# Natural feature order for x and w1, and result products dealt to four strips

## The chip, the cores and the metric

The kernel runs on one core of a Trainium2 chip. The metric is the device time in microseconds (us). The engines named below are TensorE (PE; its weight loads appear as PEld), VectorE (DVE), ScalarE (ACT), GpSimd (POOL) and SyncE (SP), which here only issues DMA transfers. The profile is one profiled execution; its times count from the start of its span.

## The reference

Two blocks follow each other. The first is a gated linear recurrence over 768 steps for 4 batches and 8 heads of 48 features; the second is a mixture of four branches of two matrix products each, on 3072 rows of 384 features.

```python
# q, k, v, alpha: (B=4, H=8, S=768, D=48)
for t in range(S):
    state = alpha[:, :, t, :, None] * state + np.einsum('bhd,bhe->bhde', k[:, :, t], v[:, :, t])
    y[:, :, t] = np.einsum('bhd,bhde->bhe', q[:, :, t], state)
x = y.transpose(0, 2, 1, 3).reshape(B * S, H * D)        # (3072, 384)

# domain_probs: (3072, 4); w1: (4, 384, 1024); w2: (4, 1024, 384)
p = domain_probs / (domain_probs.sum(-1, keepdims=True) + 1e-09)
for e in range(4):
    h = np.maximum(x @ w1[e], 0.0)
    out += p[:, e:e + 1] * (h @ w2[e])
```

All inputs and outputs are 32-bit floats. A feature of x has the number 48 h + d, with head h and position d in the head.

## The kernel before

**Units.** The sequence is cut into 6 blocks of 128 steps. One block of one batch is a unit: 24 units, ordered by block and then by batch. For a unit, `attention` loads alpha, k, q and v (128 steps on the partitions, 8 heads beside each other), transposes the first three on TensorE in pairs of heads (L277), and builds in seven levels the matrix of decayed products of queries and keys for each head, `lat` (L348 to L428). VectorE's product of q and k, L298, serves its diagonal; L307 makes the scaled queries `QT`. `result` (L436 to L471) then forms the rows of x, transposed, in the PSUM tile `yps`: for each head, values times `lat`, and, after the first block, the carried state times `QT`. `yps` has 128 partitions and three pieces of 128 columns, so 384 features by 128 steps. ScalarE copies it into the operand of the first product (L467, L471). Then TensorE multiplies keys and values (L489), and VectorE updates the state `st` (L497 to L500). The last step asks for v of the unit after next (L502).

**Result products.** Each matmul of `result` has 32 columns of weights and fills a strip of 32 partitions of `yps`; four of them in a row fill the four strips. Before the change, the 384 features are permuted: pieces 0 and 1 of `yps` hold the first 32 positions of each of the eight heads, one head to a strip, and piece 2 holds the last 16 positions of all heads, a pair of heads to a strip. For this, v of the odd heads is stored with its last 16 positions first, in tiles of 64 elements a head (`values`, L128), the rest being zeros. A piece is finished before the next one begins, and within a piece all four strips first take the state with `QT`, then the values with `lat`.

**Branches.** The units form groups: the first of 2, then five of 4, the last of 2. For each group and each of the four branches e, `up` forms x times w1 in 8 chunks of 128 hidden features, ScalarE rectifies, and `down` multiplies by w2 (L663) and adds to the sums. The first group uses raw weights in 32-bit products (L562); later groups use weights split into parts (L570). ScalarE and VectorE make the parts in the background (`split_piece`, L233 to L239), GpSimd writes them to memory (`kept`, L240), and SP loads them again for the later groups (L203).

**Loads.** `load_piece` brings a quarter of w1 of one branch, 384 rows by 256 columns, into a tile of 128 partitions and three parts (L218 to L222). Since x is permuted, the rows of w1 are too: one transfer takes the first 32 rows of heads 0 to 3, one those of heads 4 to 7, and one the last 16 rows of all heads. Quarters of w2 come in one transfer each (L224). There are 16 quarters of w1; a branch's four are asked for during the branch before it, those of the first at the start, behind the loads of the first two units. `load` brings alpha, k and q in one transfer each (L174) and v in three (L179 to L181): even heads, last 16 positions of the odd heads, first 32 positions of the odd heads. All loads go through SP's queue, in the order in which the program asks for them. Each uses one of eight semaphores in turn, so SP holds a transfer back until the one eight places before it has landed; SP also waits until the buffer to be filled has been read.

**What sets the order.** The program is laid out by hand: each engine runs its instructions in the order in which they were recorded. `advance` and `deal` mix the steps of the units into the loops over the branches by planned times; these are constants in the code. At the start, `fill` puts in matmuls on zeros, and GpSimd clears tiles (L772 to L780).

Of the kernel before, what the change touches and what calls it, by code (L numbers as in the profile page):

```python
# [10 lines left out]
F32 = mybir.dt.float32  # L11
# [9 lines left out]
def kernel(  # L21
# [37 lines left out]
    nc = tc.nc  # L59

    B, H, S, D = q.shape
    E, DM, F = moe_w1.shape
    P = 128
    NCB = S // P
    NP = H // 2
    HD = 64
    QUAD = 32
    TAIL = D - QUAD
    KC = DM // P
    FCH = F // P  # L70
    NT = B * P
    NQ = 4
    QF = F // NQ
    FPQ = FCH // NQ
    LEVELS = [1 << i for i in range(7)]
    HALF = P // 2
    assert DM == H * D and S % P == 0 and D == QUAD + HD // 4 and H == 8 and DM == 3 * P and NT <= 512 and H % 2 == 0
    assert DM % P == 0 and F % (P * NQ) == 0 and DM <= 512 and KC * QF == FPQ * DM
    FINE = 1 + 1 / 4096
    TRIM = 1 - 1 / 8192  # L80
# [3 lines left out]
    j = np.arange(P)[:, None] % HALF  # L84
    n = np.arange(QUAD)[None, :]
# [4 lines left out]
    const = ctx.enter_context(tc.tile_pool(name="const", bufs=1))  # L90
# [15 lines left out]
    lat = const.tile([P, H, P], F32, name="lat")  # L106
# [18 lines left out]
    spare = hid.tile([P, 3, 2 * NT], F32R, name="hT", bufs=NQ)  # L125
    apart = {nm: spare[:, i, :H * HD].bitcast(F32).rearrange("p (h d) -> p h d", d=HD)
             for i, nm in enumerate("akq")}
    values = [const.tile([P, H, HD], F32, name=f"rv{i}") for i in range(2)]  # L128

    blocks = [const.tile([P, NP, 2, HALF], F32, name=f"qb{i}") for i in range(4)]  # L130
    free = deque(blocks)
# [1 line left out]
    def raw(u, nm):  # L133
        return values[u % 2] if nm == "v" else apart[nm] if u == 1 else early[nm]
# [32 lines left out]
    def load(u, names):  # L167
        if u >= len(units):
            return
        cb, b = units[u]  # L170
        for nm in names:
            src = srcs[nm][b, :, cb * P:(cb + 1) * P, :].rearrange("h s d -> s h d")
            if nm != "v":
                nc.sync.dma_start(out=raw(u, nm)[:, :, :D], in_=src)  # L174
                continue

            pairs = raw(u, nm).rearrange("p (a i) d -> p a i d", i=2)
            src = src.rearrange("p (a i) d -> p a i d", i=2)
            nc.sync.dma_start(out=pairs[:, :, 0, :D], in_=src[:, :, 0])  # L179
            nc.sync.dma_start(out=pairs[:, :, 1, :TAIL], in_=src[:, :, 1, QUAD:])  # L180
            nc.sync.dma_start(out=pairs[:, :, 1, TAIL:D], in_=src[:, :, 1, :QUAD])  # L181

    kept = [[dram.tile([P, 3, KC * QF], F32, name=f"kept{l}_{i}") for i in range(E * NQ)]
# [9 lines left out]
    def load_piece(l, i, beside=False):  # L195
        if i >= E * NQ * LAST:
            return
        gi, k = divmod(i, E * NQ)
        e, c = divmod(k, NQ)
        if gi > l:  # L200
            w = wt[l][i] = wts.tile([P, 3, KC * QF], F32R, name=f"w{l + 1}",
                                    bufs=AHEAD if l == 0 else NQ)
            nc.sync.dma_start(out=w.bitcast(F32), in_=kept[l][k])  # L203
            return
        if l == 1 and not beside:
            return
        if l == 0:

            if gi > 0 or e == 0:
                shared[c] = wts.tile([P, 3, KC * QF], F32R, name="w2", bufs=NQ)  # L210
            w = shared[c][:, 2 - e % 2 if gi == 0 else 2].bitcast(F32)
        else:

            place = (hidden[c][:, 0] if not split2(gi, e, c) else hidden[c + NQ // 2][:, 1])
            w = place.rearrange("p f n -> p (f n)")[:, :KC * QF].bitcast(F32)
        wt[l][i] = w
        if l == 0:
            heads = moe_w1[e].rearrange("(h d) f -> h d f", d=D)[:, :, c * QF:(c + 1) * QF]  # L218
            w = w.rearrange("p (c f) -> p c f", f=QF)
            for part in range(2):  # L220
                nc.sync.dma_start(out=w[:, part], in_=heads[part * H // 2:(part + 1) * H // 2, :QUAD])
            nc.sync.dma_start(out=w[:, 2], in_=heads[:, QUAD:])  # L222
        else:
            nc.sync.dma_start(  # L224
                out=w.rearrange("p (c d) -> p c d", d=DM),
                in_=moe_w2[e].rearrange("(c p) d -> p c d", p=P)[:, c * FPQ:(c + 1) * FPQ])
# [53 lines left out]
    def attention(u):  # L280
        cb, b = units[u]
        ra, rk, rq, rv = (raw(u, nm) for nm in ("a", "k", "q", "v"))
# [4 lines left out]
        QT = work.tile([P, NP, P], F32, name="QT")  # L287
        nc.scalar.copy(out=AT, in_=turned(pair(ra)))
        after = u + 2 if u == 0 else u + 1 if u > 1 else len(units)
        load(after, "a")  # L290
        yield
        KT = keys()
# [3 lines left out]
        def own_terms():  # L296
            own = work.tile([P, NT], F32, name="t")[:, :H * D].rearrange("p (h d) -> p h d", d=D)
            nc.vector.tensor_mul(own, rq[:, :, :D], rk[:, :, :D])  # L298
            nc.vector.reduce_sum(out=dot, in_=own, axis=AX.X)
            load(after, "k")  # L300
# [7 lines left out]
        if alone:  # L308
            own_terms()
        load(after, "q")  # L310
        yield

# [95 lines left out]
        for r in range(NP // 2):  # L408
            for s in range(2):
                nc.tensor.matmul(far[HALF * s:HALF * (s + 1), r],  # L410
                                 lhsT=KTs[6][:, 2 * r + s, :HALF], rhs=qbs[6][:, 2 * r + s],
                                 start=True, stop=True)
# [18 lines left out]

        st = sts[b]
        flat_st = st.rearrange("p a i d -> p a (i d)")
        flat_v = rv.rearrange("p (a i) d -> p a (i d)", i=2)

        def result():  # L436
            yps = ps.tile([P, KC, P], F32, name="yps", tag="w")
            for c in range(KC):


                if c < 2:
                    now = [[(2 * c + j // 2, j % 2, (0, HD + TAIL)[j % 2], 2 * QUAD * (j % 2))
                            for j in range(4)]]
                    turns = ([(True, now[0])] if cb > 0 else []) + [(False, now[0])]
                else:
                    turns = [(True, [(p, 0, 0, QUAD) for p in range(NP)])] if cb > 0 else []
                    turns += [(False, [(p, i, QUAD + TAIL * i, 0) for p in range(NP)]) for i in range(2)]
                for n, (past, turn) in enumerate(turns):
                    for j, (p, i, in_v, in_st) in enumerate(turn):
                        nc.tensor.matmul(  # L450
                            yps[QUAD * j:QUAD * (j + 1), c, :],
                            lhsT=flat_st[:, p, in_st:in_st + QUAD] if past
                            else flat_v[:, p, in_v:in_v + QUAD],
                            rhs=QT[:, p, :] if past else lat[:, 2 * p + i, :],
                            start=(n == 0), stop=(n == len(turns) - 1))
            gi, slot = place[cb, b]
            if slot == 0:
                if gi == 0:
                    xTs[gi] = work.tile([P, 3, KC, NT], F32R, name="xT", bufs=1)
                    xraws[gi] = xTs[gi][:, 2].bitcast(F32)  # L460
                elif gi < LAST:
                    xraws[gi] = work.tile([P, KC * NT + PAD], F32, name="x_raw", bufs=1)[:, :KC * NT]
                    xraws[gi] = xraws[gi].rearrange("p (c n) -> p c n", n=NT)
                else:
                    xraws[gi] = []
            if gi < LAST:
                nc.scalar.copy(out=xraws[gi][:, :, slot * P:(slot + 1) * P], in_=yps)  # L467
            else:

                xraws[gi].append(AT)  # L470
                nc.scalar.copy(out=AT[:, :KC, :], in_=yps)  # L471
# [6 lines left out]
        for step in (turn_keys, result) if u >= half else (result, turn_keys):  # L478
            step()
            yield  # L480

        if cb < NCB - 1:
# [3 lines left out]
            for p in range(NP):  # L486
                for i in range(2) if apart_ else [slice(0, 2)]:
# [3 lines left out]
                        rhs=rv[:, 2 * p + i, :D] if apart_ else rv[:, 2 * p:2 * p + 2, :D],  # L491
                        start=True, stop=True)
# [38 lines left out]
    def up(gi, e, fc, slots=None):  # L531
# [8 lines left out]
        if fc in ((0, 2) if gi == 1 else (0,)) and begins and gi < 2:  # L540
            half = range(fc, fc + 2) if gi == 1 else range(NQ)
            for k in half:
                load_piece(1, (gi * E + e) * NQ + k, beside=True)
# [5 lines left out]
        if gi == 0 and ends and e + 1 < E and fc == (0 if e == 0 else FCH // 2):  # L549
            for k in range(NQ):  # L550
                load_piece(0, (e + 1) * NQ + k)
# [42 lines left out]
        if f == FPQ - 1 and ends:  # L594
            if gi == 0:
                for k in range(AHEAD if i == E * NQ - 1 else 0):
                    load_piece(0, i + 1 + k)
            elif gi != LAST - 1:
                del wt[0][i]
                load_piece(0, i + AHEAD)  # L600
            while late:
                load_piece(1, late.popleft())
            while stores:
                stores.popleft()()
# [164 lines left out]
    with tc.manual_schedule():  # L769
# [48 lines left out]
        for (gi, e), after in zip(tasks, [*tasks[1:], (None, None)]):  # L818
# [5 lines left out]
            turns = [range(k, k + each) for k in range(rest, len(groups[gi]), each)]  # L824
            for k, slots in enumerate(turns):

                between = deque()
                if after[1] == 0:

                    for step, at in enumerate((0.0, 0.3, 0.42, 0.54) if gi == 0 else  # L830
                                              (0.0, 0.6, 0.7, 0.78)):
                        at = at * len(turns) - k
# [33 lines left out]
```

## Time and profile before

| | |
|---|---|
| timed runs (3) | 1051.61, 1052.53, 1052.69 us; median 1052.53 |
| profiled execution | span 1050.8 us from the first to the last instruction; no other time of its own is on the page |
| granted TensorE clock | 1.000 |
| TensorE / weight loads / VectorE / ScalarE busy | 1033.8 / 899.2 / 778.3 / 565.7 us |
| result products, L450 | 768 + 480 instructions; a 32-bit matmul is two instructions |
| w1 transfers, L221 and L222 | 48 of 128 KB |
| v transfers, L179 to L181 | 24 each of 96, 32 and 64 KB |
| DMA packets | 158549, of which 120144 under 512 bytes |

Matmuls are pipelined and overlap, so the busy time of TensorE is not a sum of its instructions. A wait is put down to the engine that came last by the profile; where that engine had long been done, it was another, often a transfer. The DMA share is the mean over 16 DMA engines; it can exceed 1 a little. The time of a DMA instruction on SP includes its holding back.

### The profile page before, as it was taken

What the parts mean: (1) busy time and instruction counts of PE and PEld (TensorE: products, weight loads), DVE (VectorE), ACT (ScalarE), POOL (GpSimd) and SP (SyncE); (2) the same over time, 40 slices, a digit from 0 to 9 for tenths busy, and PEclk for the clock granted to TensorE, in tenths of its full rate; (3) what the DMA queues carried; (4) which work ended last, traced back from release to release, by engine and by line L of the source; (5) the groups of instructions that cost most, each with busy time, mean ns of one, the idle gap of its engine ahead of it and who ended that gap; (6) DMA issues with size and microseconds to landing.
All of it is one profiled execution on the core that took longest, in us unless ns stands there. A gap on an engine that the chain in (4) does not pass through costs nothing.

```text
span 1050.8 us, 21723 instructions
## 1 busy us (share of the span) xinstructions
PE 1033.8 (98%) x8554; PEld 899.2 (86%) x8554; DVE 778.3 (74%) x1620; ACT 565.7 (54%) x1195; POOL 37.7 (4%) x81
## 2 busy tenths in 40 slices
PE   8899999999999999999999999999999999999998
PEld 8777777687787899898898998898989989898998
DVE  5588777668779868778877777987887875656565
ACT  4687876575657545447456436565474453323232
POOL 3000010000001000000000000000000000000000
PEclk9999999999999999999999999999999999999999
DMA  7596699997868949669669569577594454444531
GB/s 118 161 333 210 241 313 352 320 344 235 300 247 260 382 154 317 270 210 303 241 214 336 187 219 366 183 271 258 170 361 179 183 211 180 182 184 177 207 154 46
DMA packets 158549, 251.66 MB, mean 239 GB/s; under 512 B 120144, under 2 KB 134864, under 8 KB 135920
## 3 DMA queue, kind: packets, MB, share of 16 engines
q1 hardware_dynamic: 151984, 207.89, 58.7%
q0 software_dynamic: 6016, 42.08, 10.0%
q8 instruction: 67, 1.10, 0.4%
q10 hardware_dynamic: 448, 0.32, 0.1%
q14 instruction: 34, 0.28, 0.1%
HBM read 207.79 MB, written 42.47 MB: 238 GB/s over the span
## 4 chain that ended last, share of the span: by engine, by line
PE 85%; DVE 5%; ACT 4%; DMA 2%; issue 2%; SPq 1%; POOL 0%; ACTq 0%; DVEq 0%; POOLq 0%
PE ops L663 36%; PE one L570 23%; PE two L570 11%; PE sc L355 6%; PE yps L450 3%; PE tp L277 3%; ACT qb L328 2%; PE one L562 1%; PE sps L489 1%; DMA hT<-in_moe_w_dram 1%; PE far L410 1%; DVE hT L616 1%; DMA w<-in_moe_w_dram 1%; DVE near L365 1%; DVE QT L335 1%
## 5 line engine op out<-in xcount | busy, mean ns | idle before, releaser
L663 PE MATMUL ops<-w,hT 128*128 128x384 f32 x1872 | 342.7, 340 | 0.2 <-DVE hT L616 0.2
L663 PEld LDWEIGHTS ops<-w,hT 128*128 128x128 f32 x1872 | 322.6, 188 | 4.0 <-ACT t L581 0.6
L570 PE MATMUL one<-xT,w 128*128 128x512 f32 x960 | 251.8, 398 | 0.4 <-ACT t L581 0.4
L570 PEld LDWEIGHTS one<-xT,w 128*128 128x128 f32 x960 | 176.1, 188 | 38.3 <-ACT t L581 1.2
L581 ACT ACTIVATE t<-one 128x512 f32<-128x512 f32 (+1 forms) x192 | 106.7, 556 | 175.1 <-PE one L570 169.9
L328 ACT COPY qb<-QT 64x256 f32<-64x256 f32 x336 | 136.6, 407 | 58.2 <-DVE QT L335 30.3
L610 DVE SCALAR_TENSOR_TENSOR hT<-t,hT 128x512 fp32r<-128x512 f32 (+1 forms) x172 | 110.4, 642 | 63.3 <-ACT hT L608 62.0
L583 DVE TENSOR_TENSOR t<-t,two 128x512 f32<-128x512 f32 (+1 forms) x172 | 109.2, 635 | 53.2 <-PE two L570 32.0
L608 ACT ACTIVATE hT<-t 128x512 fp32r<-128x512 f32 (+1 forms) x172 | 101.8, 592 | 86.8 <-DVE t L583 86.2
L570 PE MATMUL two<-xT,w 128*128 128x512 f32 x480 | 136.5, 393 | 0.1
L570 PEld LDWEIGHTS two<-xT,w 128*128 128x128 f32 x480 | 90.0, 188 | 20.5 <-DVE acc L692 0.9
L663 PE MATMUL ops<-hT 128*128 128x384 f32 x288 | 100.8, 492 | 0.6 <-DMA hT<-in_moe_w_dram 0.3
L616 DVE SCALAR_TENSOR_TENSOR hT<-hT 128x512 fp32r<-128x512 f32 (+1 forms) x172 | 100.6, 634 | 0.0
L365 DVE COPY_PREDICATED near<-masks,sc 128x256 f32<-128x256 uint8 x144 | 77.0, 535 | 22.2 <-PE sc L355 19.3
L335 DVE TENSOR_TENSOR QT<-QT,dec 128x256 f32<-128x256 f32 x144 | 61.0, 423 | 38.8 <-ACT qb L328 38.3
L355 PEld LDWEIGHTS sc<-qb,KT 128*64 128x64 f32 x2304 | 72.7, 138 | 9.0 <-issue 4.4
L355 PE MATMUL sc<-qb,KT 128*64 128x64 f32 x2304 | 77.2, 223 | 2.6 <-ACT qb L328 2.6
L663 PEld LDWEIGHTS ops<-hT 128*128 128x128 f32 x288 | 52.1, 190 | 30.6 <-DMA hT<-in_moe_w_dram 1.2
L692 DVE SCALAR_TENSOR_TENSOR acc<-ops,p_all,acc 128x384 f32<-128x384 f32 x82 | 49.8, 614 | 27.2 <-PE ops L663 26.3
L347 ACT COPY KT<-KT 128x256 f32<-128x256 f32 x138 | 57.5, 417 | 5.1 <-PE sc L355 1.9
L348 DVE TENSOR_TENSOR KT<-KT,dec 128x256 f32<-128x256 f32 x144 | 60.0, 417 | 0.0
L562 PE MATMUL one<-xT,w 128*128 128x256 f32 (+1 forms) x240 | 46.7, 341 | 0.6 <-ACT xT L467 0.6
(90 smaller groups left out, 932.4 us busy)
## 6 DMA issues: line engine op xcount, KB each, us to landing
w<-kept SPq DMA_DIRECT2D x144, 1152.0 KB
kept<-w POOLq DMA_DIRECT2D x32, 1152.0 KB, 7.3
hT<-in_moe_w_dram SPq DMA_DIRECT2D x32, 384.0 KB
w<-in_moe_w_dram SPq DMA_DIRECT2D x48, 128.0 KB
ra<-in_alpha_dram SPq DMA_DIRECT2D x23, 192.0 KB
rk<-in_k_dram SPq DMA_DIRECT2D x23, 192.0 KB
rq<-in_q_dram SPq DMA_DIRECT2D x23, 192.0 KB
out_dram<-acc POOLq DMA_DIRECT2D x22, 192.0 KB, 7.0
```

The source lines that it names most:

```text
L328: nc.scalar.copy(out=qb[rows, :, i, :].rearrange("p a (b r) -> p a b r", r=m), in_=qv[rows])
L335: nc.vector.tensor_mul(qv, qv, spread(dv[:, :, :, 0], m))
L348: nc.vector.tensor_mul(new[:, :, :, 0, :], old[:, :, :, 0, :], spread(halved(decs[li])[:, :, :, 1], m))
L355: nc.tensor.matmul(out[HALF * s:HALF * (s + 1), 2 * p:2 * p + 2, :], lhsT=KTs[li][:, p, HALF * s:HALF * (s + 1)], rhs=qbs[li][:, p, :, QUA ...
L365: nc.vector.copy_predicated(near.rearrange("p a (b two r) -> p a b two r", two=2, r=m)[:, :, :, 1, :], mk.unsqueeze(1).broadcast_to([P, H, ...
L570: nc.tensor.matmul(out, lhsT=w[:, part, kc], rhs=x_part(gi, part, kc), start=(part == terms[0] and kc == 0), stop=(part == terms[-1] and k ...
L581: nc.scalar.activation(out=t, in_=one, func=ACT.Copy, scale=FINE)
L583: nc.vector.tensor_add(t, t, two)
L608: nc.scalar.activation(out=top, in_=x, func=ACT.Relu, scale=TRIM)
L610: nc.vector.scalar_tensor_tensor(out=low, in0=x, scalar=0.0, in1=top.bitcast(F32), op0=ALU.max, op1=ALU.subtract)
L616: nc.vector.scalar_tensor_tensor(out=dif, in0=top.bitcast(F32), scalar=1 / 4096.0, in1=low.bitcast(F32), op0=ALU.mult, op1=ALU.subtract)
L663: nc.tensor.matmul(sums[at], lhsT=h, rhs=w, start=(n == begins[at]), stop=(n == ends[at]))
```

## The change

The features of x and the rows of w1 stand in natural order on the partitions: row 128 c + p of w1 goes to partition p of part c, and a quarter of w1 is one transfer. v is stored as it comes, in tiles of 80 elements a head (48 values and 32 zeros), and is one transfer. The 384 features are 12 blocks of 32; block 4 c + j belongs to strip j of piece c. In each pair of heads, the first block lies in the even head, the third in the odd head, and the second takes 16 positions of each; where a block takes from one head only in part, the zeros around v fill it up. So a block needs the state of its pair once and one or two products with `lat`. Each strip's products, over all three pieces, form a list, and a turn takes the next one of each strip. The number of products per unit and strip stays 4 without and 7 with a state.

```diff
-    TAIL = D - QUAD
+    VD = D + QUAD
...
-    values = [const.tile([P, H, HD], F32, name=f"rv{i}") for i in range(2)]
+    values = [const.tile([P, H, VD], F32, name=f"rv{i}") for i in range(2)]
...
-            if nm != "v":
-                nc.sync.dma_start(out=raw(u, nm)[:, :, :D], in_=src)
-                continue
-
-            pairs = raw(u, nm).rearrange("p (a i) d -> p a i d", i=2)
-            src = src.rearrange("p (a i) d -> p a i d", i=2)
-            nc.sync.dma_start(out=pairs[:, :, 0, :D], in_=src[:, :, 0])
-            nc.sync.dma_start(out=pairs[:, :, 1, :TAIL], in_=src[:, :, 1, QUAD:])
-            nc.sync.dma_start(out=pairs[:, :, 1, TAIL:D], in_=src[:, :, 1, :QUAD])
-
+            nc.sync.dma_start(out=raw(u, nm)[:, :, :D], in_=src)
...
-            heads = moe_w1[e].rearrange("(h d) f -> h d f", d=D)[:, :, c * QF:(c + 1) * QF]
-            w = w.rearrange("p (c f) -> p c f", f=QF)
-            for part in range(2):
-                nc.sync.dma_start(out=w[:, part], in_=heads[part * H // 2:(part + 1) * H // 2, :QUAD])
-            nc.sync.dma_start(out=w[:, 2], in_=heads[:, QUAD:])
+            nc.sync.dma_start(
+                out=w.rearrange("p (c f) -> p c f", f=QF),
+                in_=moe_w1[e].rearrange("(c p) f -> p c f", p=P)[:, :, c * QF:(c + 1) * QF])
...
-        flat_v = rv.rearrange("p (a i) d -> p a (i d)", i=2)
+        flat_v = rv.rearrange("p h d -> p (h d)")
 
         def result():
             yps = ps.tile([P, KC, P], F32, name="yps", tag="w")
+            strips = [[] for _ in range(P // QUAD)]
             for c in range(KC):
-
-
-                if c < 2:
-                    now = [[(2 * c + j // 2, j % 2, (0, HD + TAIL)[j % 2], 2 * QUAD * (j % 2))
-                            for j in range(4)]]
-                    turns = ([(True, now[0])] if cb > 0 else []) + [(False, now[0])]
-                else:
-                    turns = [(True, [(p, 0, 0, QUAD) for p in range(NP)])] if cb > 0 else []
-                    turns += [(False, [(p, i, QUAD + TAIL * i, 0) for p in range(NP)]) for i in range(2)]
-                for n, (past, turn) in enumerate(turns):
-                    for j, (p, i, in_v, in_st) in enumerate(turn):
-                        nc.tensor.matmul(
-                            yps[QUAD * j:QUAD * (j + 1), c, :],
-                            lhsT=flat_st[:, p, in_st:in_st + QUAD] if past
-                            else flat_v[:, p, in_v:in_v + QUAD],
-                            rhs=QT[:, p, :] if past else lat[:, 2 * p + i, :],
-                            start=(n == 0), stop=(n == len(turns) - 1))
+                for j, strip in enumerate(strips):
+                    p, part = divmod(len(strips) * c + j, 3)
+                    terms = [(flat_st[:, p, QUAD * part:QUAD * (part + 1)], QT[:, p, :])] if cb > 0 else []
+                    for i in range(2):
+                        if part != 2 * (1 - i):
+                            at = VD * (2 * p + i) + QUAD * part - D * i
+                            terms.append((flat_v[:, at:at + QUAD], lat[:, 2 * p + i, :]))
+                    strip += [(c, n == 0, n == len(terms) - 1, *term) for n, term in enumerate(terms)]
+            for turn in zip(*strips):
+                for j, (c, begins, ends, lhsT, rhs) in enumerate(turn):
+                    nc.tensor.matmul(yps[QUAD * j:QUAD * (j + 1), c, :], lhsT=lhsT, rhs=rhs,
+                                     start=begins, stop=ends)
```

More of the change, by code (lines that the diff above doesn't have):

```diff
@@ L76 @@
     HALF = P // 2
-    assert DM == H * D and S % P == 0 and D == QUAD + HD // 4 and H == 8 and DM == 3 * P and NT <= 512 and H % 2 == 0
+    assert DM == H * D and S % P == 0 and 2 * D == 3 * QUAD and H == 8 and DM == 3 * P and NT <= 512 and H % 2 == 0
     assert DM % P == 0 and F % (P * NQ) == 0 and DM <= 512 and KC * QF == FPQ * DM
```

## The prediction

> **What bounds the kernel now.** I read the page first, for the busy shares and the slices, then the list of waits of TensorE, then busy time by stretch, then the timeline around the stalls that a transfer can have caused, and the chain for the result products. From the page, the line of the engines and the slices of the DMA:
>
> ```profile
> PE 1033.8 (98%) x8554; PEld 899.2 (86%) x8554; DVE 778.3 (74%) x1620; ACT 565.7 (54%) x1195; POOL 37.7 (4%) x81
> DMA  7596699997868949669669569577594454444531
> ```
>
> TensorE is idle for 17.0 us of 1050.8. By stretch, 12 of them lie before 160 us and 4.2 behind 1000; between 165 and 1000 us it waits for less than 1 us. So a transfer can give time back only in the first 160 us, and only where TensorE really stands. The larger waits of TensorE there (us in total, times, longest):
>
> ```profile
> PE yps L450 <- ACT lat L428: 2.8, 3, 1.4
> PE sc L355 <- ACT qb L328: 2.6, 3, 1.2
> PE far L410 <- ACT qb L328: 0.8, 1, 0.8
> PE sps L489 <- ACT AT L475: 0.6, 1, 0.6
> PE yps L450 <- DVE QT L307: 0.5, 1, 0.5
> PE tp L277 <- ACT hT L564: 0.4, 1, 0.4
> PE ops L663 <- DMA hT<-in_moe_w_dram: 0.3, 1, 0.3
> ```
>
> Most are waits for ScalarE, and no wait of ScalarE for a transfer is listed. Next, four stretches (columns: length, then busy time of PE, PEld, DVE, ACT, POOL, granted clock, DMA share, GB/s). In the first two only raw w1 is on its way; the third and fourth carry w2 quarters and kept pieces:
>
> ```profile
> 16.00:24.00 8.00, 6.67 (x100) 6.23 (x103) 7.61 (x22) 3.71 (x9) 0.64 (x2) 1.00 0.34 108
> 42.00:49.00 7.00, 6.84 (x73) 5.53 (x72) 0.00 (x0) 4.33 (x11) 0.00 (x0) 1.00 0.34 112
> 144.00:150.00 6.00, 6.00 (x33) 5.39 (x32) 3.56 (x9) 5.43 (x12) 0.53 (x1) 1.00 1.10 403
> 150.00:154.00 4.00, 3.85 (x14) 2.10 (x13) 3.97 (x9) 3.96 (x10) 0.53 (x1) 1.00 1.05 371
> ```
>
> Raw w1 moves at 108 to 112 GB/s with two thirds of the DMA engines' time empty; other loads reach 403. The timeline shows where this meets TensorE (start, length, what; in brackets the idle time before it):
>
> ```profile
> 113.32 1.16 SPq L221 DMA_DIRECT2D w<-in_moe_w_dram  x2
> ...
> 128.64 1.30 SPq L222 DMA_DIRECT2D w<-in_moe_w_dram  x1
> 130.03 0.53 SPq L174 DMA_DIRECT2D rq<-in_q_dram  x1
> 136.90 0.56 DVE L298 TENSOR_TENSOR t<-rq,rk 128x384 f32<-128x384 f32 x1 [2.43 <-DMA rq<-in_q_dram]
> 136.94 0.63 PE L277 MATMUL tp<-ident,rq 128*128 128x128 f32 x4 [0.44 <-ACT hT L564]
> 140.34 0.68 DVE L307 TENSOR_TENSOR QT<-tp,AT 128x512 f32<-128x512 f32 x1
> 141.08 0.43 PE L450 MATMUL yps<-QT,st 128*32 128x128 f32 x8 [0.48 <-DVE QT L307]
> 153.11 0.30 PEld L663 LDWEIGHTS ops<-hT 128*128 128x128 f32 x2 [0.76 <-DMA hT<-in_moe_w_dram]
> ```
>
> One load of q stands on SP's queue behind twelve w1 transfers, which took it from 113.32 to 129.94. It lands about 136.90: VectorE's product of q and k and TensorE's transposes of q start together then, so the 0.44 us put down to ScalarE is this load too. VectorE, 2.43 us late, reaches QT late, and the result products wait 0.48. At 153.11 a w2 quarter, issued behind all this, is late.
>
> **The change part by part.**
>
> *w1 in one transfer.* 48 transfers become 16. A quarter (393 KB) takes 3.5 us at 108 to 112 GB/s. The nearest row for the new form is the w2 quarter: the same bytes, its partitions outermost, moved in a stretch at 403 GB/s, so 0.98 us; its four issues took 2.17 us at 30.37 and 4.85 at 138.56. The last batch of w1 thus takes 4 to 7 us of SP instead of 16.6, and q goes out 9 to 12 us earlier; its buffer was free once VectorE had read it, at 110.6. That removes 0.44 and, with QT 2.4 us earlier, 0.48. The w2 batch at 138.56 stands behind a load of k that waits for VectorE's product at 136.90. This now comes at 134.5, when VectorE is done with the split before it, so w2 goes out about 2.4 us earlier, with a shorter backlog in front. The stall at 153.11 is 0.15 us in the busy time of its row (3.85 of 4.00), 0.30 by the spacing of the matmuls. I take 0.15, since ScalarE and VectorE are full there (3.96 and 3.97 of 4.00) and would hold TensorE back next. Earlier stalls for a transfer are worth nothing. 0.39 us of weight loads waited for w1 at 30.0 and 30.5, but the state products at 31.64 wait 0.6 for ScalarE, which has no gap. The 0.34 for w2 at 35.83 is followed at 38.87 by 0.84 for ScalarE. Both merely lengthen the next wait.
>
> The Trainium skill, page "DMA: Bandwidth & Descriptors", section "Why a DMA increments its semaphore by 16 and not by 1", says that the slowest dimension of each access pattern fixes how many of the 16 DMA engines share a transfer. By it the old transfers, with 4, 4 and 8 heads outermost, use 4, 4 and 8 of them, the new one all 16: an estimate from that page of (3/16) / (1/4 + 1/4 + 1/8) = 0.30 for the share before, beside 0.34 in the trace. The sum by the rule is the sum by the row.
>
> *What the single transfer costs.* The first matmul on a quarter now waits for all 393 KB rather than for a third. The bound is the time of the other two thirds: 0.65 us at 403 GB/s, per batch that is only just in time. Only the batch used from 25 us on was (30.0 and 30.5); it now has several us in hand. I take 0; the end is +0.65. The same section of that page says that an intermediate count of the semaphore doesn't tell which bytes have landed, so no early start is left. That rule speaks against the change and puts the sum at the +0.65 end if a quarter comes just in time; nothing before shows one landing whole.
>
> *v in one transfer.* 72 issues become 24, and 1536 small packets a unit become 1024. In the steady part the three issues take 0.38, 0.46 and 0.51 us of SP; TensorE waits there for no transfer, so this is 0. Were that cover gone, the saving of about 1 us a unit would count as gain, so the bound has no loss in it. At the start, clearing the wider value tiles takes 640/512 of 0.52 us each, 0.26 for both. GpSimd's next work for others, a copy at 8.12, had 1.54 us of idle time before it. The first v goes out 0.13 later (3.30 instead of 3.17), then SP is freed about 1.1 us sooner. Cost 0; without the cover 0.26.
>
> *Result products dealt out.* There are 16 (first blocks) or 28 matmuls per unit as before, four in a turn on the four strips, in the same strip order; products of QT and of lat, and different pieces of the result, now share a turn. The chain shows such bursts (start, us):
>
> ```profile
> 99.21 1.01 PE yps L450 x32
> 187.60 1.67 PE yps L450 x56
> ```
>
> Four turns take 1.01, seven 1.67, so 0.22 a turn. The turns of the first blocks already stream four different lat tiles, and a switch from QT to lat between turns costs nothing in the timeline. The first product on lat still comes behind one turn of QT. I take 0. One end is one more turn's time for each of the 20 long bursts, 4.4 us; the other is a gain of 0, as a strip can't be more than full.
>
> **Sum.** 0.44 + 0.48 + 0.15 = 1.07 us off the profiled execution: span 1050.8 to 1049.7. The timed runs are 1051.61 to 1052.69, so 0.8 to 1.9 us lie around the span; the median 1052.53 goes to 1051.4.
>
> **The rivals.**
>
> *Nothing arrives.* The saved 0.92 is spent in the next wait for ScalarE, busy 5.43 of 6.00 us from 144 to 150. So it is also if w1 still moves at 110 GB/s. Against the first: TensorE has no wait from 141.5 to 153. Time 1052.3.
>
> *More goes than I count.* If the attention steps behind the stalls at 78.48 (1.20), 82.35 (1.21) and 119.60 (1.45) are late through their loads in a way that the list does not name, up to 3.9 us more go: 1052.53 - 1.07 - 3.9 = 1047.6, half of it 1049.5. For: SP is blocked by w1 from 72.9 to 89.1 and from 113.3 to 129.9. Against: ScalarE and VectorE show no transfer wait there.
>
> *Slower: the mixed turns.* If a turn whose strips take different operands overlaps less, each long burst of 28 matmuls pays. One more turn time each, 20 x 0.22 = 4.4, less 1.07, is 1055.9. It decides from 0.16 us a burst (2.1 + 1.07 over 20). For: no row of before mixes QT and lat within a turn. Against: the equal 0.22 above.
>
> **How the numbers follow.** 0.2% is 2.1 us, about what a measurement of this kernel tells from no change. The forecast (0.5 to 1.6 us gained) gets 0.47 and nothing arrives 0.16, both within 0.2%. More goes gets 0.24, mixed turns 0.13. Faster 0.26 (the third case and 0.02 of the first), same 0.61, slower 0.13. The range reaches from 1049.0, just below the half-way value of the third case, to 1053.2, which is 1052.53 plus the 0.65 of the single transfer; the slower case and the far third lie outside, about 0.2. The forecast's own range is 1050.9 to 1052.0.
>
> **What would show it.** The DMA share and GB/s while w1 loads: 108 to 112 now, above 250 if the first step is right. The last w1 batch: 16.6 us on SP, then under 8. At 137 and 141 us no wait of TensorE, and VectorE's product before 135. Bursts of 1.01 and 1.67 us unchanged. ScalarE's stalls at 78, 82 and 120 still there. I am wrong if those go too, if a burst gets longer, or if TensorE meets a new wait for w1 at 25 to 35 us.

## The result, and the profile after

| | before | after |
|---|---|---|
| timed runs (20 each), median | 1052.47 us (1051.28 to 1055.91) | 1050.96 us (1050.21 to 1052.20) |
| profiled execution, span | 1050.8 us | 1049.6 us |

The ratio of after to before is 0.9987, with a 95% interval of 0.9981 to 0.9993: 1.4 us or 0.13% faster, inside the 0.2% that the prediction called "same". The forecast was 1051.4. The medians and ratios here are of executions at the full granted clock: one execution of before_q_first, 1278.15 us at a granted clock of 0.75, is left out, and its trace was taken in a second run, before_q_first_look.

From the page of the kernel after, the line of the engines and the slices of the DMA. TensorE is busy for 1.3 us less with the same number of instructions and idle for 17.1 us, as before. A matmul that waits for its operand while others are passing counts as busy, so these totals do not tell where the time went; the stretches do.

```profile
PE 1032.5 (98%) x8554; PEld 898.8 (86%) x8554; DVE 778.2 (74%) x1620; ACT 565.6 (54%) x1195; POOL 37.9 (4%) x81
DMA  9397789887868948768669559577595454444531
```

The list of waits of TensorE after the change (us in total, times, longest). The lines for the transposes of q, for QT and for the late w2 quarter are gone. The waits for `lat` and for `qb` at `sc` stay; those for `qb` at `far` and for `AT` have grown, from 0.8 and 0.6 to 1.2 each. Two lines are new, a wait for a kept piece and one for VectorE's sum `acc`.

```profile
PE yps L439 <- ACT lat L417: 2.8, 3, 1.4
PE sc L344 <- ACT qb L317: 2.6, 3, 1.2
...
PE far L399 <- ACT qb L317: 1.2, 1, 1.2
...
PE sps L474 <- ACT AT L460: 1.2, 1, 1.2
...
PE one L555 <- DMA w<-kept: 0.4, 1, 0.4
...
PE ops L648 <- DVE acc L677: 0.3, 1, 0.3
```

The same stretches as before, in the same columns (length, busy PE, PEld, DVE, ACT, POOL, granted clock, DMA share, GB/s). From 16 to 24 us, where w1 moved at 108 GB/s with a share of 0.34, the share is now 1.10; the 264 GB/s there are not w1's alone, since alpha, k, q and w2 follow it in this stretch. From 36 to 40 us, which was not among them, only the second batch of w1 is on its way, at 276 GB/s. From 42 to 49 us nothing is left to move. From 150 to 154 us TensorE is busy throughout (3.85 before).

```profile
16.00:24.00 8.00, 6.49 (x105) 5.78 (x103) 7.41 (x23) 3.69 (x9) 0.40 (x1) 1.00 1.10 264
36.00:40.00 4.00, 2.75 (x44) 1.94 (x43) 2.28 (x9) 2.49 (x7) 0.00 (x0) 1.00 0.82 276
42.00:49.00 7.00, 6.96 (x76) 6.08 (x76) 0.59 (x1) 4.36 (x10) 0.00 (x0) 1.00 0.01 2
...
144.00:150.00 6.00, 6.00 (x27) 4.82 (x26) 5.47 (x13) 5.78 (x13) 0.53 (x1) 1.00 1.05 403
150.00:154.00 4.00, 4.00 (x56) 2.74 (x56) 3.93 (x8) 3.93 (x10) 0.53 (x1) 1.00 1.08 363
```

The timeline of the kernel after, around the stalls (start, length, what). The last batch of w1 takes SP 3.18 us, q is asked for at 113.67 instead of 130.03, and VectorE's product at 133.65, the transposes of q and the products on QT follow without a wait. The last line has the new wait.

```profile
110.40 3.18 SPq L209 DMA_DIRECT2D w<-in_moe_w_dram  x4
113.67 0.44 SPq L173 DMA_DIRECT2D rq<-in_q_dram  x1
133.65 0.55 DVE L287 TENSOR_TENSOR t<-rq,rk 128x384 f32<-128x384 f32 x1
135.60 0.60 PE L266 MATMUL tp<-ident,rq 128*128 128x128 f32 x4
137.09 0.68 DVE L296 TENSOR_TENSOR QT<-tp,AT 128x512 f32<-128x512 f32 x1
139.16 0.43 PE L439 MATMUL yps<-QT,st 128*32 128x128 f32 x8
162.30 1.62 PE L555 MATMUL one<-xT,w 128*128 128x512 f32 x6 [0.43 <-DMA w<-kept]
```

The chain, for the bursts of result products: as long as before, 1.01 and 1.67 us.

```profile
98.48 1.01 PE yps L439 x32
...
185.80 1.67 PE yps L439 x56
```

One table is used for all kernels below. It holds distances in us between starts on TensorE, from the timelines: from the first product on w1 (near 24 us) to the result products on `lat` near 119; from these to the transposes of q; to the first products on QT; to the transposes of the next alpha (near 152); to the first product on a kept piece (near 162); to the next burst on QT (near 186).

| kernel | w1 to 119 | to q | to QT | to alpha | to kept | to 186 |
|---|---|---|---|---|---|---|
| before | 94.49 | 17.34 | 4.14 | 12.78 | 10.24 | 23.43 |
| before_again | 94.47 | 17.11 | 4.14 | 12.98 | 10.50 | 23.43 |
| after | 94.47 | 16.74 | 3.56 | 12.36 | 10.78 | 23.43 |
| after_again | 94.51 | 16.74 | 3.56 | 12.37 | 10.04 | 23.49 |
| w1_thirds | 94.48 | 16.74 | 3.56 | 12.36 | 10.25 | 23.43 |
| v_thirds | 94.47 | 16.73 | 3.56 | 12.37 | 9.89 | 23.64 |
| piece_by_piece | 94.51 | 16.76 | 3.56 | 12.39 | 10.25 | 23.46 |
| before_q_first_look | 94.45 | 16.73 | 3.57 | 12.36 | 10.99 | 23.43 |
| after_q_first | 94.49 | 16.74 | 3.56 | 12.36 | 10.37 | 23.46 |

So the change takes 0.60, 0.58 and 0.42 us out of three neighbouring distances, 1.60 in all, and nothing before 119 us. In this one profile 0.54 goes back at the kept piece, and 0.5 more behind 186 us.

### The profile page after: what moved, and what is told of

Its sections match the earlier page's. It is cut to its first block, busy times and chain, and to the rows that moved or that the text cites. A ratio compares the mean times of both kernels' runs of the same rounds, so it can differ in the third digit from the quotient of the medians.

```text
span 1049.6 us, 21621 instructions
## 1 busy us (share of the span) xinstructions
PE 1032.5 (98%) x8554; PEld 898.8 (86%) x8554; DVE 778.2 (74%) x1620; ACT 565.6 (54%) x1195; POOL 37.9 (4%) x81
## 4 chain that ended last, share of the span: by engine, by line
PE 86%; DVE 5%; ACT 5%; DMA 2%; issue 2%; POOL 0%; SPq 0%; ACTq 0%; DVEq 0%; POOLq 0%
PE ops L648 35%; PE one L555 23%; PE two L555 11%; PE sc L344 6%; PE yps L439 3%; PE tp L266 3%; PE one L547 2%; ACT qb L317 2%; PE sps L474 1%; PE far L399 1%; DMA w<-kept 1%; DVE near L354 1%; DMA rq<-in_q_dram 1%; PE idle L780 1%; DVE hT L601 1%
```

## The experiments

**The kernel after, once more (after_again).** No edit.

> The changed kernel once more, as the yardstick for the three beside it. Theory A (w1's share of the DMA engines and its slots on SP's queue): about 1.4 us faster than before (0.9987); no wait of TensorE at 137 and 139 us, a wait of about 0.4 for a kept piece at 162. The start of the profile tells a second thing: in the changed kernel's profile the first products of the first group began at 24.39 us, before 25.11. Theory S (the start gains because v and w1 take fewer places on the queue): again 24.4 within 0.1. Theory N (it is variation of the start): another value between 24.3 and 25.2.

Measured: 1051.07 us, ratio 0.9990 (0.9982 to 0.9999), span 1048.6. The three distances are those of after; the wait for the kept piece is not there (10.04). So the 1.60 us belong to the kernel, and that wait varies from one execution to the next. The first product on w1 starts at 24.07 us, outside what either theory on the start gave (24.3 to 24.5 us, or another value up to 25.2); the last section comes back to it.

**w1 over fewer DMA engines (w1_few_engines).** Natural order as in after, but 124 partitions in three transfers and the other four in one.

```diff
+            w = w.rearrange("p (c f) -> p c f", f=QF)
+            src = moe_w1[e].rearrange("(c p) f -> p c f", p=P)[:, :, c * QF:(c + 1) * QF]
-            nc.sync.dma_start(
-                out=w.rearrange("p (c f) -> p c f", f=QF),
-                in_=moe_w1[e].rearrange("(c p) f -> p c f", p=P)[:, :, c * QF:(c + 1) * QF])
+            for part in range(KC):
+                nc.sync.dma_start(out=w[:124, part], in_=src[:124, part])
+            nc.sync.dma_start(out=w[124:], in_=src[124:])
```

> The changed kernel, but with w1 again on few DMA engines, in natural order: per quarter three transfers of 124 partitions and one of 4. Theory A: w1 moves at 100 to 120 GB/s again, the last batch holds SP for 14 to 18 us, and the waits at 137 to 141 (0.44 and 0.48 before) and for w2 at 152 come back, the wait at 162 goes: 0.7 to 1.4 us slower than the changed kernel, near the kernel before. Rival (the number of v transfers or the dealing carries the gain): as the changed kernel within 0.3 us.

Measured: 1061.64 us, ratio 1.0085 (1.0071 to 1.0099), span 1059.6. It was meant to bring the time of before back, and went 9 us past it; its last batch of w1 holds SP for 19.7 us (16.6 in before). From the windows of this kernel, the stretch in which only w1 is on its way, and from its timeline the transposes of q:

```profile
42.00:49.00 7.00, 6.85 (x76) 4.91 (x72) 1.19 (x3) 3.20 (x8) 0.00 (x0) 1.00 0.28 97
```
```profile
144.76 1.09 PE L268 MATMUL tp<-ident,rq 128*128 128x128 f32 x4 [6.26 <-DMA rq<-in_q_dram]
```

The same bytes in nearly the same layout move at 97 GB/s, with a share of 0.28, because of four partitions left out of each transfer; and the wait named is the one that the prediction had found, the load of q, now 6.26 us long. The trace also records when the semaphore of a load is increased. A w1 transfer that has landed has added 16 to it in after, 5, 5 and 9 in before (4, 4 and 8 heads outermost), and 5 here, with 124 partitions and with 4. The Trainium skill, page "DMA: Bandwidth & Descriptors", section "Why a DMA increments its semaphore by 16 and not by 1", says that the number of engines is the largest one up to 16 that divides the slowest dimension of both access patterns; by it 124 partitions give 4, an estimate of 0.25 for the share, and 128 give 16. The 0.28 here agrees, and so does the share of after while w1 is alone, 0.99 from 36 to 39 us.

Why it is worse than before has several parts in the trace. From the first product on w1 to the burst at 119 us (here 121.60) it takes 97.48 us, 3.0 more than before: the last transfer of the first batch of w1 lands at 31.33 us, and TensorE stands 2.58 us for it until 31.43. Measured from the burst, q is asked for 3.8 us later than before (135.79 - 121.60 = 14.19 against 130.03 - 119.60 = 10.43), and it then takes 2.1 us longer to be used (8.97 against 6.91). Last, the granted clock falls to 0.50 while TensorE stands for q, and stays there until 148.11 us:

```profile
141.30:148.00 6.70, 3.24 (x10) 2.82 (x11) 3.21 (x5) 0.00 (x0) 0.00 (x0) 0.50 0.64 157
```

The transposes of q then take 1.09 us instead of 0.63, and from them to the products on QT it is 5.23 us instead of 4.14. These are 9.9 us of loss. The span is 8.8 us longer than that of before, since this execution starts 1.0 us earlier and has no stall at 152 us (0.4), and loses 0.3 after it.

The same records show why q is used so late once it is asked for. Twelve of the 16 increments of its semaphore come from 138.31 to 138.78 us, the other four from 144.47 to 144.62. In before they come from 132.92 to 133.39 and from 136.41 to 136.80, in after all from 120.67 to 122.13. A quarter of q is late, then, which fits four of the 16 engines that are still busy with w1; the rest of q is not held up.

**The same with half the transfers (w1_slow_whole).** Two transfers a quarter, 124 and 4 partitions, to tell whether the number of transfers behind q or the bytes on few engines set the delay.

```diff
-            for part in range(KC):
-                nc.sync.dma_start(out=w[:124, part], in_=src[:124, part])
+            nc.sync.dma_start(out=w[:124], in_=src[:124])
             nc.sync.dma_start(out=w[124:], in_=src[124:])
```

> The changed kernel, with w1 on few DMA engines as in the run with four transfers a quarter, but in two transfers a quarter, of 124 and 4 partitions, so that the batch takes 8 places on SP's queue instead of 16. If the places on the queue make q late (theory P): SP is through the last batch in under 10 us although w1 still moves at about 100 GB/s, q goes out before 122 us, and no wait of TensorE above 0.3 us comes at 134 to 146; the time is within 0.7 us of the changed kernel. If the bytes on few engines make it late (theory E), since q needs those engines too: q lands at about 137 us or later whatever SP does, the wait at 134 to 146 is back, and the time is 0.7 us or more above the changed kernel.

Measured: 1063.63 us, ratio 1.0103 (1.0088 to 1.0119), span 1062.1. From its timeline:

```profile
136.08 0.39 SPq L173 DMA_DIRECT2D rq<-in_q_dram  x1
...
145.50 1.09 PE L267 MATMUL tp<-ident,rq 128*128 128x128 f32 x4 [6.82 <-DMA rq<-in_q_dram]
```

Half as many transfers did not bring q forward: it is asked for at 136.08 against 135.79, and the wait is 6.82. The rate is the same (98 GB/s from 42 to 49 us). So the bytes on few engines set the delay, not the places on the queue. The trace says so too: SP is held 6.66 us by the transfer that it issues at 125.23, though the one eight places before had landed at 117.27; and in before, every w1 transfer was issued 0.8 us or more after the one eight places before it had landed. The holding of SP in these batches is therefore not the wait for that place; what holds it was not found out.

**Three transfers, all partitions (w1_thirds).** One third of the quarter each, over all 128 partitions.

```diff
+            for part in range(KC):
+                nc.sync.dma_start(out=w[:, part], in_=src[:, part])
```

> The changed kernel, with each quarter of w1 in three transfers again, one per part, each over all 128 partitions. It tells the number of transfers from their spread over the engines. If the spread carries it (theory A1): above 250 GB/s while w1 loads, the last batch on SP for under 9 us, time as the changed kernel within 0.3 us. If the number of transfers carries it, through the eight places of the queue (theory A2): the batch holds SP for 12 us or more and at least 0.5 us of the gain is lost.

Measured: 1050.74 us, ratio 0.9987 (0.9978 to 0.9996), span 1049.2. Its last batch is 8.97 us on SP instead of 3.18, q is asked for at 120.11, and all three distances are those of after. From 36 to 40 us, where w1 is alone, it moves at 203 GB/s (276 in after). So the single transfer is faster but worth nothing in time here: what counts is that all the partitions are outermost. It also bounds the price that the prediction asked about: waiting for the whole quarter instead of a third costs nothing either.

**The kernel before, with q ahead of w1 (before_q_first, and before_q_first_look for the trace).** w1 and v as before; the last batch of w1 is asked for one chunk later, so that the load of q goes out first.

```diff
-        if gi == 0 and ends and e + 1 < E and fc == (0 if e == 0 else FCH // 2):
+        if gi == 0 and ends and e + 1 < E and fc == (0 if e == 0 else FCH // 2 + (e == 2)):
```

> The kernel before, with one thing moved: the last batch of w1 is asked for one chunk of the products later, so that the load of q that stood behind it goes out ahead of it; all transfers keep their form. Theory A: the waits at 137 and 141 us (0.44 and 0.48) go and w2 is no earlier, or later, so that up to 0.5 us may come back at 153: 0.4 to 0.9 us faster than before. Rival (those two waits are ScalarE's, as the list of waits puts them): no change, within 0.2 us.

> The same kernel as in the run with q ahead of the last batch of w1, for its trace: no wait of TensorE for the transposes of q and for QT at 134 to 142 us; w2 is issued behind w1 and lands later than in the kernel before or at the same time, so that a wait for it near 152 stays or grows.

Measured: 1051.16 us (median of ten), ratio 0.9990 (0.9981 to 0.9999); the second run 1051.12, span 1049.2. From its timeline:

```profile
112.61 0.53 SPq L174 DMA_DIRECT2D rq<-in_q_dram  x1
...
128.19 1.29 SPq L222 DMA_DIRECT2D w<-in_moe_w_dram  x1
...
135.50 0.60 PE L277 MATMUL tp<-ident,rq 128*128 128x128 f32 x4
```

w1 is as slow as ever (115 GB/s from 42 to 49 us, SP held until 129.48), yet all three distances are those of after: 16.73, 3.57, 12.36. One constant in the order of the loads gives what the change gives. The stall at 152 us was expected to stay or grow, and it went. So it, too, is a consequence of the late q, through the load of k and the w2 batch behind it (asked for at 136.81 instead of 138.56), and needs no faster w1.

**Both together (after_q_first).** The same edit on the kernel after.

> The kernel after, with its last batch of w1 asked for one chunk later, so that the load of q goes out ahead of it (the same edit that gave the kernel before 1051.42 us). Theory one cause: both edits remove the same delay, that of the load of q behind a slow batch of w1, so together they give what each gives alone, 1050.8 to 1051.5 us, ratio 0.998 to 0.9995; the spacing from the result products at 119 us to the transposes of q stays 16.7 us, from there to the products on QT 3.6 us, and from there to the transposes of the next alpha 12.4 us. Theory two causes (the w1 rate gives something of its own, the place of q something else): the gains add, 2 x 1.1 to 1.5 us below the kernel before, 1049.4 to 1050.2 us, and at least one of the three spacings gets shorter by 0.3 us or more.

Measured: 1050.97 us, ratio 0.9986 (0.9977 to 0.9995), span 1048.9; distances 16.74, 3.56, 12.36. The gains do not add: one cause.

**v in three transfers (v_thirds).** Natural order, the rest as after.

```diff
+            pairs = raw(u, nm).rearrange("p (a i) d -> p a i d", i=2)
+            src = src.rearrange("p (a i) d -> p a i d", i=2)
+            nc.sync.dma_start(out=pairs[:, :, 0, :D], in_=src[:, :, 0])
+            nc.sync.dma_start(out=pairs[:, :, 1, :D - QUAD], in_=src[:, :, 1, :D - QUAD])
+            nc.sync.dma_start(out=pairs[:, :, 1, D - QUAD:D], in_=src[:, :, 1, D - QUAD:])
```

> The changed kernel, with v in three transfers again (natural order, packets of 192, 64 and 128 bytes as before). Theory A: v carries none of the gain; within 0.4 us of the changed kernel, the batch of w1 on SP under 5 us, TensorE without a wait at 134 to 146. The rival that v's transfers hold SP: 0.5 us or more of the gain is lost.

Measured: 1051.42 us, ratio 0.9991 (0.9982 to 0.9999), span 1048.7. The median is 0.46 us above that of after and 0.35 above that of after_again, less than the intervals can tell apart. No distance of the table up to 152 us moves, and the first product on w1 starts at 24.36 against 24.39. The single transfer of v is worth nothing that can be measured.

**Each piece finished before the next (piece_by_piece).** The products of the kernel after, in turns that stay within one piece of the result: nine turns instead of seven, some with empty places.

```diff
-            for turn in zip(*strips):
-                for j, (c, begins, ends, lhsT, rhs) in enumerate(turn):
+            pieces = [[[term for term in strip if term[0] == c] for strip in strips] for c in range(KC)]
+            for turn in (turn for piece in pieces for turn in zip_longest(*piece)):
+                for j, term in enumerate(turn):
+                    if term is None:
+                        continue
+                    c, begins, ends, lhsT, rhs = term
```

> The changed kernel with the same result products, but each of the three pieces of the result finished before the next begins: a piece then needs 3 turns where a state is used 2 or 3 products a strip, and in its third turn (second for the first blocks a second one) only one or two strips have work. Theory T (a turn costs 0.22 us whether its strips are full or not): 9 turns a long burst instead of 7, so 2.1 us instead of 1.67 for 20 bursts and 6 instead of 4 for the first four: 9 to 11 us slower. Rival (strips run on by themselves and the order is free): long bursts of 1.7 us, time within 1 us of the changed kernel.

Measured: 1051.48 us, ratio 0.9992 (0.9983 to 1.0001), span 1049.1. From its chain:

```profile
184.97 1.69 PE yps L444 x56
```

The theory that every turn costs 0.22 us falls. Nine turns would be 9 x 0.22 = 1.98 us, and the burst takes 1.69, 0.02 more than with seven. Each strip runs through its own seven products without waiting for a turn to be full. That a burst lasts as long as its fullest strip fits this, but was not shown: in all the kernels here the four strips have the same number of products.

**The kernel before, once more (before_again).** No edit.

> The kernel before, once more, for its profile. If the stalls are properties of the program: spacings of 17.3, 4.1 and 12.8 us from the result products at 119 us to the transposes of q, to the products on QT and to the next transposes, within 0.1 us, and a late load of w2 near 153 us. If the start moves by the run and not by the change: the first product on w1 starts anywhere between 24.0 and 25.1 us, as in the profiles so far; if it belongs to the kernel, at 25.1 us.

Measured: 1052.26 us, span 1050.2. The stalls come back: 17.11, 4.14 and 12.98, together 34.23 us as against 34.26 in before and 32.66 in after. How the loss is shared between q and w2 moves by 0.2 us, more than the 0.1 that was expected; the sum does not move. This time the list names the load of q itself. From the timeline of before_again:

```profile
135.68 0.63 PE L277 MATMUL tp<-ident,rq 128*128 128x128 f32 x4 [0.21 <-DMA rq<-in_q_dram]
```

The first product on w1 starts at 24.10, against 25.11 in before with the same instructions: the start moves by the run, as one of the two theories on it had said; what it goes by is in the last section.

## Why the prediction was right

*The place and the cause.* The prediction named one load of q behind twelve transfers of w1, with VectorE, QT and a w2 batch behind it. With w1 slower this wait grew more than any other (to 6.26 and 6.82 us), and moving q alone removed all of it. It did not ask why q, once asked for, took another 6.9 us to be used; in before the last four of its 16 increments come 3 us behind the others. Here the forecast held step by step: rate 108 to above 250 GB/s (276 in after and 251 in after_again, from 36 to 40 us), 16.6 us on SP to under 8 (3.18), VectorE's product before 135 (133.65), no wait at 137 and 141.

*The sizes.* Forecast 0.44 + 0.48 + 0.15 = 1.07 us; the distances give 0.60 + 0.58 + 0.42 = 1.60. The first two terms were the idle times in brackets. These start at the modelled end of the matmul before, and a matmul's record is longer than the distance to the next start (0.27 us against 0.11 for the transposes), so they show less than the time lost; the distance between starts, set against the same distance where nothing is late, shows it whole. Only after the result was there such a second distance. The third term was mis-sized by a choice: the spacing of the matmuls gave 0.30, and 0.15 was taken since ScalarE and VectorE looked full and "would hold TensorE back next". They did not; 0.42 went, and 0.62 in the execution of before_again. Engines busy for 3.96 of 4 us were not the next limit there. That the total came so near is in part luck: 0.5 us more went than was forecast, and about as much was lost behind 186 us, which the prediction did not expect.

*What was given back.* The prediction asked what would be late next only for w2, and did not see the kept pieces. TensorE now waits for one near 162, 0.43 us in after and 0.64 in before_q_first_look. The DMA share is 1.05 and 1.08 in the stretches before it, so that the writes of the split pieces and the loads that read them back are probably the next limit; this was argued, not tried. It is not a fixed price: the distance to the kept piece is 10.24 and 10.50 in the two profiles of before and 9.89 to 10.99 in those of the other kernels of the table. Later still, from the burst at 186 us to the end, after takes 863.8 us and before 863.3 and 863.4. Part of it is the new wait for VectorE's sum `acc`, 0.30 us at 334.96 in after; the burst near 350 us is then 0.2 us late. The kernels after, after_again, after_q_first and piece_by_piece have this wait, all of them with w1 and v in one transfer each; v_thirds, w1_thirds and the kernels with the old transfers do not. Why `acc` is late there was not settled.

*What was costed at nothing.* The early waits: from the first product on w1 to 119 us all kernels of the table agree within 0.06 us, although before waits twice for w1 at 30 us and once for w2 at 35.83 and after does not. The wait at the state products grew instead from 0.61 to 1.16, and the one for `qb` at 38 from 0.84 to 1.25, as the prediction had said. The single transfer (end +0.65), v (end 0.26) and the dealing (end 4.4) cost nothing: w1_thirds, v_thirds and the bursts of 1.67 show it. For the dealing the value was right and its reason wrong: there is no time per turn, so there was none to add.

*The rivals.* "Nothing arrives" fell with the gain in the three distances. "More goes" fell with the waits for `lat` and `qb` at 78, 82 and 120, which stand as before, and "mixed turns" with the bursts.

*The profiles against the times.* The spans of the two first profiles differ by 1.2 us. That is not the 1.60 less something small: 0.72 of it is the start (25.11 against 24.39), which moves by as much between the two profiles of before (25.11 and 24.10); 1.06 is the stretch from 119 to 186, and some 0.5 is lost behind it. The profiles of before_again and after_again, which start 0.03 us apart, differ by 1.6. The medians, 1.5 us apart, carry the result; the distances say where it comes from.

## What to carry to other kernels

When one engine is fed by a single queue of loads, ask for each small load what large ones stand in front of it, and try the order before the rate: here one constant was worth as much as a new layout. Put the partitions outermost in a transfer, and all 128 of them; where w1 was alone it then moved at 203 GB/s in three transfers and 251 to 276 in one, instead of 104 to 118 in the old form, and 95 to 98 with 124 partitions. Size a stall by the distance between starts, compared with the same stretch undisturbed, rather than by the idle time in brackets, and ask what the earlier work runs into.

## What was not expected of the hardware

TensorE's first matmuls take different times in executions of the same program. The first transposes of the kernel before, from its timeline in before and then in before_again (start, length of four transposes):

```profile
4.68 1.09 PE L277 MATMUL tp<-ident,ra 128*128 128x128 f32 x4
6.41 1.02 PE L277 MATMUL tp<-ident,rk 128*128 128x128 f32 x4
7.94 0.60 PE L277 MATMUL tp<-ident,rq 128*128 128x128 f32 x4
```
```profile
4.39 0.63 PE L277 MATMUL tp<-ident,ra 128*128 128x128 f32 x4
5.75 0.63 PE L277 MATMUL tp<-ident,rk 128*128 128x128 f32 x4 [0.28 <-DMA rk<-in_k_dram]
6.92 0.63 PE L277 MATMUL tp<-ident,rq 128*128 128x128 f32 x4
```

Four transposes take 1.09 or 0.63 us at 4 to 5 us from the start, and 0.60 to 0.63 from 7 us on; the slow start ends 1.0 us later. The views give a granted clock of 1.00 throughout, but a stretch for which the trace has no record counts as 1.00 there, and the records of the clock begin only at 7.27 us in before and at 4.20 in before_again. In the eleven traces other than that of before_q_first, matmuls in close order start 0.21 us apart up to the first record and 0.11 apart behind it. Where the records give 0.50, after the long wait in w1_few_engines, four transposes take 1.09 us as well. So TensorE most likely starts at half the clock, and the time at which the full clock is granted is what differs. The first product on w1 starts at 24.96 to 25.11 us where the records begin at 7.27 to 7.42 (before, w1_thirds, w1_slow_whole), and at 23.97 to 24.39 where they begin at 4.20 to 6.19 (the other eight). The start belongs to the execution and not to the change; what makes the full clock come sooner or later is not shown. A comparison of two single profiles of a kernel with a start like this can be off by 1 us for this reason alone.

The other is that 124 partitions instead of 128 in a transfer took the rate of w1 from 276 to 97 GB/s, and the time of a load behind it from no wait to 6 us, enough to turn a gain of 1.4 us into a loss of 9.
